# Two last token chunks of a linear map go through the weights together, and one block of stored weight combinations is dropped

## The chip, the cores and the metric

The kernel runs on one NeuronCore of a Trainium2 chip. TensorE (PE in the profile) multiplies, VectorE (DVE) and ScalarE (ACT) empty its PSUM banks and prepare operands, GpSimd (POOL) does a little elementwise work, and SyncE (SP) issues every DMA. The metric is the device time in microseconds (us); less is better.

## The reference, cut to what matters

Three parts follow each other: an attention that is linear in the sequence, a first mixture of plain matrix products, and a second mixture of four experts.

```python
# attention, 4 batches x 8 heads x 576 x 64; x becomes 2304 tokens x 512
q_s, k_s = softmax(q, axis=-1), softmax(k, axis=2)
x = einsum(q_s, einsum(k_s, v))
# first mixture: w1, w2 512x1024, w3 1024x1024, w_out 1024x512
x = ((x @ w1) * (x @ w2)) @ w3 @ w_out
# second mixture: 4 experts, w1 4x512x1024, w2 4x1024x512
p = domain_probs / domain_probs.sum(-1)
out = sum(p[:, e] * (relu(x @ w1[e]) @ w2[e]) for e in range(4))
```

## The kernel before, in words

Every fp32 operand of a product is held as two halves, a rounded high part and the rest (`split`: ScalarE writes the high part, L102, then VectorE the low part, L103), and each product is three matmuls (`mm3`, L107 to L109).

**First mixture.** The 2304 tokens are cut into five chunks, 0 to 3 of 512 tokens and 4 of 256. The 1024 inner columns are cut into NF = 8 slices f. `ab_step(c, f)` computes the two products of chunk c with slice f of w1 and w2, 12 matmuls each, into two banks of the pool `ps_w`; ScalarE copies the first out (L476, tile `ah`) and VectorE multiplies the second onto it (L477). `h_step` splits that product. `y_step(c, f)` multiplies it with slice f of `Wg` = w3 @ w_out into four accumulators `y`, 12 matmuls; these live in the four banks of the pools `ps_y`. `y_out(c)` copies them out at the end of a chunk (L508) and stores them in DRAM as `yd` (L511). The products of chunks 0 and 1 are computed early, between attention work; their `y_step`s run in 16 slots from Y0. Chunks 2, 3 and 4 follow, each with eight slices of `ab_step`, `h_step` and the `y_step` of the slice before; attention work of the last batch is put between the slices of chunk 2. The split slices of w1 and w2 are kept in DRAM, and `load_w12(c, f)` reads them again (tile `wg`, two DMAs of 512 KB, L447) for each chunk from 1 on, two slices ahead. They come from the pool `gran` of 28 buffers, which also holds x, h, ah, yt and Wg.

**Second mixture.** It is computed in three passes over the tokens, each of NGE = 8 blocks n (an expert's half of the inner columns). A block's two layers use a seven-product scheme: `layer1(n)` has 84 matmuls of 384 columns (L847) in seven steps, `layer2(n)` 126 of 256 columns (L921). The seven right-hand combinations of each layer's weights (e_a, e_s for layer 1, e_b, e_t for layer 2) are formed once. Those of layer 2, and of layer 1 for the blocks n < NE1, are formed ahead by the generator `cooking`, whose steps are taken by `cook_some(k)` during the first mixture: a block's raw weights come in by two DMAs (`load_e`, L573, tiles e1r and e2r), eleven steps make seven combinations (tiles `eo`, NOUT = 5 buffers; sums on L577, splits on L102 and L103), and each is stored in DRAM (L597). `load_cooked` reads them back (tile `eg`, pool of 9 buffers, L658). For the other blocks of layer 1, `get_e1(n)` forms the combinations in the first pass itself, among the work of the layer before, from raw weights held in `rp2`, and stores them for the later passes. `load_y` and `tset` prepare the left-hand token combinations of a pass (tiles yp and t). The pool `rp2` is opened after `gran` is closed, as are the other pools of the second mixture but yp, tok and e.

**Order.** The program is traced in the order in which the Python runs, which gives each instruction its priority. A planner then fixes the order on every engine at build time from its own timeline; it may move an instruction ahead of earlier ones if its inputs and a buffer are there. On the chip each engine and the SP queue work through their list in that fixed order.

Of the kernel before, what the change touches and what calls it, by code (L numbers as in the profile page):

```python
# [11 lines left out]
ACTF = mybir.ActivationFunctionType  # L12
# [3 lines left out]
PSUM = bass.MemoryType.PSUM  # L16
# [15 lines left out]
AB0, AB1, W1, Y0, Y1, REST = 6, 14, 22, 30, 38, 46  # L32
# [22 lines left out]
def linear_attention_moe_kernel(ctx: ExitStack, tc, q, k, v, w1, w2, w3, wo, dp, e1, e2, out):  # L55
    nc = tc.nc
# [3 lines left out]
    NF = w1.shape[1] // 256  # L60
    E = e1.shape[0]
    P = 128
# [2 lines left out]
    chunks = [(j, min(CH, NT - j)) for j in range(0, NT, CH)]  # L65
    NC = len(chunks)
    KR, KX = 4, S - 4 * P
    NE1, NOUT = 2, 5
    QP, QR = 64, 9
    HALF = S // 2  # L70
    NG, NR = 28, 4
# [10 lines left out]
    ps_y = [ctx.enter_context(tc.tile_pool(name=f"ps_y{i}", bufs=2, space=PSUM)) for i in range(2)]  # L82
    ps_w = ctx.enter_context(tc.tile_pool(name="ps_w", bufs=2, space=PSUM))

    def gran(name):
        return gp.tile([P, 2, 512], F32R, tag="g", name=name)

    def raw(name, pool=gp):
        return pool.tile([P, 1024], F32, tag="g", name=name)

    def bank(pool, name):
        return pool.tile([P, 512], F32, tag="b", name=name)
# [8 lines left out]
    def split(hi, lo, src, eng=nc.vector):  # L101
        i = nc.scalar.activation(out=hi, in_=src, func=ACTF.Copy)  # L102
        eng.tensor_tensor(out=lo, in0=src, in1=hi.bitcast(F32), op=ALU.subtract)  # L103
        return i

    def mm3(ps, w_hi, w_lo, r_hi, r_lo, first, last):
        nc.tensor.matmul(out=ps, lhsT=w_hi, rhs=r_hi, start=first, stop=False)  # L107
        nc.tensor.matmul(out=ps, lhsT=w_hi, rhs=r_lo, start=False, stop=False)  # L108
        nc.tensor.matmul(out=ps, lhsT=w_lo, rhs=r_hi, start=False, stop=last)  # L109

    gate = {}

# [47 lines left out]
    att = ExitStack()  # L160
# [189 lines left out]
    before, mid, after = {}, {}, {}  # L350

    def put(d, slot, f, *a):
        d.setdefault(slot, []).append((f, a))

    def run(d, slot):
        for f, a in d.pop(slot, []):
            f(*a)

    for b in range(B):
        for j in range(2):  # L360
            s = Q_SLOT[b][j]
# [6 lines left out]
        for i, hp in enumerate(PAIRS):  # L368
            s = K_SLOT[b][i]
# [17 lines left out]
    w12, w12d = {}, {}  # L387
# [56 lines left out]
    def load_w12(c, f):  # L444
        for i in range(2):
            g = gran("wg")
            gate["dma"] = [nc.sync.dma_start(out=g.bitcast(F32), in_=w12d[f, i])]  # L447
            w12.setdefault((c, f), []).append(g)

    def finish_lo(g, ps):  # L450
        nc.tensor.matmul(
            out=ps, lhsT=nident, rhs=g[:, 0], start=False, stop=True, skip_group_check=True
        )
        nc.scalar.activation(out=g[:, 1], in_=ps, func=ACTF.Copy)


    hg, yps, Wg, prods = {}, {}, {}, {}

    def ab_step(c, f):
        n = chunks[c][1]  # L460
        gw = w12[c, f]
        pss = []
        if f % 2 == 0:
            prods[c, f // 2] = gp.tile([P, 2, 512], F32, tag="g", name="ah")
        ah = prods[c, f // 2][:, f % 2, 0:n]
        for i in range(2):
            ps = bank(ps_y[i] if c == 0 and f % 2 else ps_w, "ab")
            for x, kt in enumerate(PAIRS):
                o = P * kt
                mm3(  # L470
                    ps[:, 0:n], gw[i][:, 0, o:o + P], gw[i][:, 1, o:o + P],
                    xa.at(c, kt, 0), xa.at(c, kt, 1), x == 0, x == KT - 1,
                )
            pss.append(ps)
            if i == 0:
                nc.scalar.activation(out=ah, in_=ps[:, 0:n], func=ACTF.Copy)  # L476
        nc.vector.tensor_tensor(out=ah, in0=pss[1][:, 0:n], in1=ah, op=ALU.mult)  # L477


    def h_step(c, f):  # L480
        n = chunks[c][1]
        h = gran("h")
        split(h[:, 0, 0:n], h[:, 1, 0:n], prods[c, f // 2][:, f % 2, 0:n])
        if f % 2:
            del prods[c, f // 2]
        hg[c, f] = h

    def y_step(c, f):
        n = chunks[c][1]
        if f == 0:  # L490
            for d in range(KT):
                yps[d] = bank(ps_y[d // 2], f"y{d}")
        h = hg.pop((c, f))
        for d in range(KT):
            o = P * d
            mm3(
                yps[d][:, 0:n], Wg[f][:, 0, o:o + P], Wg[f][:, 1, o:o + P],
                h[:, 0, 0:n], h[:, 1, 0:n], f == 0, f == NF - 1,
            )

    yd = dr.tile([P, KT, NT], F32, name="yd")
# [1 line left out]
    def y_out(c):  # L503
        j0, n = chunks[c]
        for dd in range(2):
            t = raw("yt").rearrange("p (k f) -> p k f", k=2)
            for k in range(2):
                nc.scalar.activation(  # L508
                    out=t[:, k, 0:n], in_=yps[2 * dd + k][:, 0:n], func=ACTF.Copy
                )  # L510
            nc.sync.dma_start(out=yd[:, 2 * dd:2 * dd + 2, j0:j0 + n], in_=t[:, :, 0:n])  # L511

    def x_free(c):
        for kk in list(xa.t):
            if kk[0] == c:
                del xa.t[kk]
# [59 lines left out]
    def minus(dst, x, y, op=ALU.subtract):  # L576
        return lambda: nc.vector.tensor_tensor(out=dst, in0=x, in1=y, op=op)  # L577
# [52 lines left out]
    def load_y(p):  # L630
        y = yp_.tile([P, KT, 2, TC], F32, tag="yp", name="yp")
        nc.sync.dma_start(
            out=y, in_=yd[:, :, 2 * TC * p:2 * TC * (p + 1)].rearrange("p k (t n) -> p k t n", t=2)
        )
        yraw[p] = y

    def tset(p):
        y = yraw.pop(p)
        b11, b12, b21, b22 = y[:, 0:2, 0], y[:, 0:2, 1], y[:, 2:4, 0], y[:, 2:4, 1]
        t = tok[p] = {}  # L640

        def part(name, src):
            def do():
                t[name] = tp.tile([P, 2, 2, TC], F32R, tag="t", name="t")
                split(t[name][:, :, 0], t[name][:, :, 1], src)
            return do

        return [
            part("b11", b11), part("b21", b21),
            minus(b11, b12, b11), minus(b12, b22, b12),  # L650
            part("b22", b22), minus(b22, b22, b11),
            part("t2", b22), part("t1", b11), part("t3", b12),
            minus(b21, b21, b22), part("t4", b21),
        ]

    def load_cooked(kind, n, name):
        g = ep.tile([P, 2, 2, 256], F32R, tag="e", name="eg")
        nc.sync.dma_start(out=g.bitcast(F32), in_=ewd[kind, n % NGE, name])  # L658
        ew[kind, n, name] = g

    def slot(s, *steps):
        run(before, s)
        for f, *args in steps:
            f(*args)
            run(mid, s)
        run(mid, s)
        run(after, s)
# [49 lines left out]
    save_w12(NF - 2)  # L717
    save_w12(NF - 1)
    load_w12(1, 0)
    load_w12(1, 1)  # L720
    for f in range(NF):
        if f + 2 < NF:
# [14 lines left out]
    kitchen = ExitStack()  # L737
# [3 lines left out]
    def cook_some(k):  # L741
        for _ in range(k):
            next(cooks, None)

    for i, (c, f) in enumerate(steps):
        if c == 1 and f >= NF - 2:
            load_w12(2, f - NF + 2)
        if i + 4 < len(steps):
            h_step(*steps[i + 4])
        slot(Y0 + i, (y_step, c, f))  # L750
        cook_some(2)
        if f == NF - 1:
            y_out(c)


    put(before, REST + NF * (NC - 4), load_probs)
    put(after, REST + NF * (NC - 4) + 2, probs)
    for c in range(2, NC):
        for f in range(NF):
            s = NF * (c - 2) + f  # L760
            if s < NF * (NC - 2) - 2:
                load_w12((s + 2) // NF + 2, (s + 2) % NF)
            run(before, REST + s)
            ab_step(c, f)
            h_step(c, f)
            cook_some(3)
            run(mid, REST + s)
            if f > 0:
                y_step(c, f - 1)
            cook_some(2)  # L770
            run(after, REST + s)
        x_free(c)
        y_step(c, NF - 1)
        y_out(c)
        if c == NC - 3:
            att.close()
            yp_ = ctx.enter_context(tc.tile_pool(name="yp", bufs=1, side="right"))
            tp = ctx.enter_context(
                tc.tile_pool(name="tok", bufs=7, side="right", reuse_waits="tile")
            )  # L780
        if c == NC - 2:
            cook_some(200)
            kitchen.close()
            load_y(0)
            for g in tset(0):
                g()
            ep = ctx.enter_context(
                tc.tile_pool(name="e", bufs=9, side="right", reuse_waits="tile")
            )
            for name in USE["e1"]:  # L790
                load_cooked("e1", 0, name)
    gran_stack.close()
    Wg.clear()

# [238 lines left out]
```

## Time and profile before

| what | value |
|---|---|
| median of 3 runs | 1186.36 us (1184.99 to 1188.56) |
| profiled execution | 1184.92 us, of which the span from first to last instruction is 1183.1 us |
| granted TensorE clock, mean | 0.991 |
| PE busy | 1130.7 us (96% of the span), 7048 matmuls |
| PE weight loads | 1051.4 us (89%) |
| DVE busy | 866.8 us (73%) |
| ACT busy | 535.8 us (45%) |
| DMA | 322.18 MB, mean 272 GB/s |

Busy shares are means over the whole span. A matmul's shown duration is longer than its distance to the next one, since matmuls are pipelined; the pace is read from the starts. What an idle engine waited for is inferred from semaphores.

### The profile page before, as it was taken

To read this page: it belongs to the slowest core of one execution; us is meant where nothing else is said; L and a number is where in the kernel's file an instruction comes from. 1 tells how busy PE (TensorE), PEld (TensorE's weight loads), DVE (VectorE), ACT (ScalarE), POOL (GpSimd) and SP (SyncE) were. 2 spreads that over 40 slices of the span, in tenths; PEclk is the share of its full clock that TensorE was granted. 3 is DMA by queue.
4 is the path that set the end of the run, shared out by engine and by line. 5 is a ranking of instruction groups with operands and counts; after the bars stand their busy time and mean duration, and the time that the engine had idled before them with its cause. 6 is when DMAs were issued, how large, how long until landed. Compare 5 with 4: busy or idle time off the path is not lost.

```text
span 1183.1 us, 18802 instructions
## 1 busy us (share of the span) xinstructions
PE 1130.7 (96%) x7048; PEld 1051.4 (89%) x7048; DVE 866.8 (73%) x1428; ACT 535.8 (45%) x982; POOL 50.5 (4%) x70
## 2 busy tenths in 40 slices
PE   5889999989998998999999999999999999999997
PEld 3667888778787898999999999999999999999997
DVE  6997867776467421799989987777779777777776
ACT  4665535555435322555555554434445344443441
POOL 0011300012001000000000000000000000000000
PEclk9989999999999999999999999999999999999999
DMA  9999950699899985778786789777777787777773
GB/s 231 266 350 298 361 204 21 246 365 412 305 392 344 367 337 204 270 285 286 276 288 252 257 290 316 263 251 250 249 250 244 258 297 257 251 251 251 247 252 99
DMA packets 130730, 322.18 MB, mean 272 GB/s; under 512 B 32336, under 2 KB 53328, under 8 KB 130640
## 3 DMA queue, kind: packets, MB, share of 16 engines
q1 hardware_dynamic: 130640, 320.98, 78.9%
q8 instruction: 56, 0.92, 0.3%
q14 instruction: 34, 0.28, 0.1%
HBM read 244.39 MB, written 76.55 MB: 271 GB/s over the span
## 4 chain that ended last, share of the span: by engine, by line
PE 81%; DMA 8%; DVE 5%; SPq 2%; ACT 2%; issue 1%; DVEq 0%; ACTq 0%
PE hp L847 29%; PE op L921 27%; PE ab L107 5%; PE ab L109 4%; PE ab L108 4%; DMA kr<-in_k_dram 2%; PE y L108 2%; PE y L107 2%; PE y L109 2%; DVE acc L905 1%; DMA eg<-e_a 1%; PE kv L244 1%; PE W L107 1%; PE W L108 1%; PE W L109 1%
## 5 line engine op out<-in xcount | busy, mean ns | idle before, releaser
L921 PE MATMUL op<-eg,h 128*128 128x256 f32 x3024 | 377.5, 280 | 1.4 <-DMA eg<-e_b 1.3
L847 PE MATMUL hp<-t,eg 128*128 128x384 f32 x2016 | 373.8, 336 | 2.3 <-DMA eg<-e_a 1.7
L921 PEld LDWEIGHTS op<-eg,h 128*128 128x128 f32 x3024 | 371.5, 188 | 1.9 <-issue 1.6
L847 PEld LDWEIGHTS hp<-t,eg 128*128 128x128 f32 x2016 | 345.0, 188 | 3.7 <-ACT blk L836 1.8
L905 DVE SCALAR_TENSOR_TENSOR acc<-op,prob,acc 128x256 f32<-128x256 f32 (+1 forms) x396 | 196.5, 525 | 45.8 <-PE op L921 45.4
L102 ACT ACTIVATE h<-blk 128x768 fp32r<-128x768 f32 x168 | 137.8, 842 | 142.7 <-DVE blk L577 108.8
L103 DVE TENSOR_TENSOR h<-blk,h 128x768 fp32r<-128x768 f32 x168 | 157.1, 949 | 26.9 <-ACT h L102 26.9
L830 ACT ACTIVATE blk<-hp 128x384 f32<-128x384 f32 x192 | 91.2, 490 | 147.7 <-PE hp L847 145.6
L107 PE MATMUL ab<-x,wg 128*128 128x512 f32 (+1 forms) x320 | 123.0, 386 | 8.7 <-DMA wg<-w 4.0
L834 DVE TENSOR_TENSOR blk<-hp,blk 128x384 f32<-128x384 f32 x144 | 79.5, 555 | 69.8 <-PE hp L847 67.5
L108 PE MATMUL ab<-x,wg 128*128 128x512 f32 (+1 forms) x320 | 120.8, 377 | 0.2 <-ACT x L346 0.2
L109 PE MATMUL ab<-x,wg 128*128 128x512 f32 (+1 forms) x320 | 120.2, 378 | 0.6 <-DVE wg L103 0.6
L836 ACT ACTIVATE blk<-blk 128x768 f32<-128x768 f32 x72 | 60.8, 846 | 74.1 <-DVE blk L834 72.3
L577 DVE TENSOR_TENSOR blk<-blk 128x768 f32<-128x768 f32 x96 | 91.2, 950 | 0.6
L107 PEld LDWEIGHTS ab<-x,wg 128*128 128x128 f32 x320 | 62.0, 195 | 20.3 <-DMA wg<-w 4.2
L109 PEld LDWEIGHTS ab<-x,wg 128*128 128x128 f32 x320 | 61.7, 193 | 11.7 <-DVE wg L103 1.3
L108 PEld LDWEIGHTS ab<-x,wg 128*128 128x128 f32 x320 | 62.1, 194 | 11.0 <-ACT x L346 1.2
L103 DVE TENSOR_TENSOR eo<-e2r,eo 128x512 fp32r<-128x512 f32 x56 | 39.2, 706 | 40.7 <-ACT eo L102 40.7
L477 DVE TENSOR_TENSOR ah<-ab,ah 128x512 f32<-128x512 f32 (+1 forms) x40 | 25.4, 634 | 52.2 <-PE ab L109 43.1
L108 PE MATMUL y<-h,W 128*128 128x512 f32 (+1 forms) x160 | 58.4, 372 | 3.3 <-DVE h L103 3.3
L109 PE MATMUL y<-h,W 128*128 128x512 f32 (+1 forms) x160 | 57.7, 371 | 0.0
L107 PE MATMUL y<-h,W 128*128 128x512 f32 (+1 forms) x160 | 52.0, 373 | 1.0 <-ACT h L102 1.0
(91 smaller groups left out, 1010.4 us busy)
## 6 DMA issues: line engine op xcount, KB each, us to landing
eg<-e_t SPq DMA_DIRECT2D x96, 512.0 KB, 4.7
eg<-e_s SPq DMA_DIRECT2D x72, 512.0 KB, 4.5
eg<-e_b SPq DMA_DIRECT2D x72, 512.0 KB, 5.1
wg<-w SPq DMA_DIRECT2D x64, 512.0 KB, 9.4
eg<-e_a SPq DMA_DIRECT2D x54, 512.0 KB, 4.8
f<-in_moe_w_dram SPq DMA_DIRECT2D x32, 512.0 KB, 6.7
e_t<-eo SPq DMA_DIRECT2D x32, 512.0 KB, 7.5
e_b<-eo SPq DMA_DIRECT2D x24, 512.0 KB, 8.6
```

The costliest lines, as they stand in the source:

```text
L102: i = nc.scalar.activation(out=hi, in_=src, func=ACTF.Copy)
L103: eng.tensor_tensor(out=lo, in0=src, in1=hi.bitcast(F32), op=ALU.subtract)
L107: nc.tensor.matmul(out=ps, lhsT=w_hi, rhs=r_hi, start=first, stop=False)
L108: nc.tensor.matmul(out=ps, lhsT=w_hi, rhs=r_lo, start=False, stop=False)
L109: nc.tensor.matmul(out=ps, lhsT=w_lo, rhs=r_hi, start=False, stop=last)
L577: return lambda: nc.vector.tensor_tensor(out=dst, in0=x, in1=y, op=op)
L830: nc.scalar.activation(out=block(name)[:, u], in_=src, func=func)
L834: nc.vector.tensor_tensor(out=x[:, u], in0=src, in1=x[:, u], op=ALU.add)
L836: nc.scalar.activation(out=x, in_=x, func=ACTF.Relu)
L847: nc.tensor.matmul(out=q, lhsT=w[:, sw, kt, P * u:P * u + P], rhs=t[b][:, kt, st], start=new and kt == 0 and i == 0, stop=kt == 1 and i == ...
L905: nc.vector.scalar_tensor_tensor(out=dst, in0=src, scalar=prob[:, T, e:e + 1], in1=dst, op0=ALU.mult, op1=ALU.add,)
L921: nc.tensor.matmul(out=q[:, c:c + DH], lhsT=g[:, sh, u, P * i:P * i + P], rhs=w[:, sw, u], start=new and u == 0 and j == 0, stop=u == 1 an ...
```

## The change

Three things. (1) Chunks 3 and 4 go through the slices together: `load_w12` is called for chunk 3 alone and its buffers are used by `ab_step(3, f)` and `ab_step(4, f)`, then come `y_step(3, f - 1)` and `y_step(4, f - 1)`. Chunk 4's four accumulators are pairs of halves of two banks of a new PSUM pool `ps_z`, opened when the attention's pool is closed. (2) NE1 is 1: block 1's layer-1 combinations are no longer stored ahead, but formed during `layer1(0)` like those of the blocks after it, and the raw weights of blocks 1 and 2 are the first two reads into `rp2`. (3) The steps of `cook_some` are spread otherwise: none in the first three slots from Y0, four a slice in chunk 2 and eight a slice in the joint chunks; the kitchen is closed at slice 5 of the joint chunks, and yp, tok and e are opened there, with `tset(0)` dealt out over slices 5 to 7 and the first seven `load_cooked` at slice 6.

```diff
@@ -65,7 +65,7 @@
     chunks = [(j, min(CH, NT - j)) for j in range(0, NT, CH)]
     NC = len(chunks)
     KR, KX = 4, S - 4 * P
-    NE1, NOUT = 2, 5
+    NE1, NOUT = 1, 5
     QP, QR = 64, 9
     HALF = S // 2
     NG, NR = 28, 4
@@ -103,10 +103,11 @@
         eng.tensor_tensor(out=lo, in0=src, in1=hi.bitcast(F32), op=ALU.subtract)
         return i
 
-    def mm3(ps, w_hi, w_lo, r_hi, r_lo, first, last):
-        nc.tensor.matmul(out=ps, lhsT=w_hi, rhs=r_hi, start=first, stop=False)
-        nc.tensor.matmul(out=ps, lhsT=w_hi, rhs=r_lo, start=False, stop=False)
-        nc.tensor.matmul(out=ps, lhsT=w_lo, rhs=r_hi, start=False, stop=last)
+    def mm3(ps, w_hi, w_lo, r_hi, r_lo, first, last, shared=False):
+        kw = {"skip_group_check": True} if shared else {}
+        nc.tensor.matmul(out=ps, lhsT=w_hi, rhs=r_hi, start=first, stop=False, **kw)
+        nc.tensor.matmul(out=ps, lhsT=w_hi, rhs=r_lo, start=False, stop=False, **kw)
+        nc.tensor.matmul(out=ps, lhsT=w_lo, rhs=r_hi, start=False, stop=last, **kw)
 
     gate = {}
 
@@ -446,6 +447,8 @@
             g = gran("wg")
             gate["dma"] = [nc.sync.dma_start(out=g.bitcast(F32), in_=w12d[f, i])]
             w12.setdefault((c, f), []).append(g)
+        if c == NC - 2:
+            w12[NC - 1, f] = w12[c, f]
 
     def finish_lo(g, ps):
         nc.tensor.matmul(
@@ -454,7 +457,7 @@
         nc.scalar.activation(out=g[:, 1], in_=ps, func=ACTF.Copy)
 
 
-    hg, yps, Wg, prods = {}, {}, {}, {}
+    hg, yps, Wg, prods, ps_z = {}, {}, {}, {}, []
 
     def ab_step(c, f):
         n = chunks[c][1]
@@ -487,15 +490,21 @@
 
     def y_step(c, f):
         n = chunks[c][1]
-        if f == 0:
+        pair = c == NC - 1
+        if f == 0 and pair:
+            for dd in range(2):
+                t = bank(ps_z[0], f"z{dd}")
+                for k in range(2):
+                    yps[c, 2 * dd + k] = t[:, 256 * k:256 * k + n]
+        elif f == 0:
             for d in range(KT):
-                yps[d] = bank(ps_y[d // 2], f"y{d}")
+                yps[c, d] = bank(ps_y[d // 2], f"y{d}")[:, 0:n]
         h = hg.pop((c, f))
         for d in range(KT):
             o = P * d
             mm3(
-                yps[d][:, 0:n], Wg[f][:, 0, o:o + P], Wg[f][:, 1, o:o + P],
-                h[:, 0, 0:n], h[:, 1, 0:n], f == 0, f == NF - 1,
+                yps[c, d], Wg[f][:, 0, o:o + P], Wg[f][:, 1, o:o + P],
+                h[:, 0, 0:n], h[:, 1, 0:n], f == 0 and not (pair and d % 2), f == NF - 1, pair,
             )
 
     yd = dr.tile([P, KT, NT], F32, name="yd")
@@ -506,7 +515,7 @@
             t = raw("yt").rearrange("p (k f) -> p k f", k=2)
             for k in range(2):
                 nc.scalar.activation(
-                    out=t[:, k, 0:n], in_=yps[2 * dd + k][:, 0:n], func=ACTF.Copy
+                    out=t[:, k, 0:n], in_=yps[c, 2 * dd + k], func=ACTF.Copy
                 )
             nc.sync.dma_start(out=yd[:, 2 * dd:2 * dd + 2, j0:j0 + n], in_=t[:, :, 0:n])
 
@@ -748,47 +757,67 @@
         if i + 4 < len(steps):
             h_step(*steps[i + 4])
         slot(Y0 + i, (y_step, c, f))
-        cook_some(2)
+        if i > 2:
+            cook_some(2)
         if f == NF - 1:
             y_out(c)
 
 
-    put(before, REST + NF * (NC - 4), load_probs)
-    put(after, REST + NF * (NC - 4) + 2, probs)
-    for c in range(2, NC):
-        for f in range(NF):
-            s = NF * (c - 2) + f
-            if s < NF * (NC - 2) - 2:
-                load_w12((s + 2) // NF + 2, (s + 2) % NF)
-            run(before, REST + s)
+    put(before, REST + NF, load_probs)
+    put(after, REST + NF + 2, probs)
+    for f in range(NF):
+        load_w12((f + 2) // NF + 2, (f + 2) % NF)
+        run(before, REST + f)
+        ab_step(2, f)
+        h_step(2, f)
+        cook_some(2)
+        run(mid, REST + f)
+        if f > 0:
+            y_step(2, f - 1)
+        cook_some(2)
+        run(after, REST + f)
+    x_free(2)
+    y_step(2, NF - 1)
+    y_out(2)
+    att.close()
+    two = ExitStack()
+    ps_z.append(two.enter_context(tc.tile_pool(name="ps_z", bufs=2, space=PSUM)))
+    for f in range(NF):
+        if f + 2 < NF:
+            load_w12(3, f + 2)
+        run(before, REST + NF + f)
+        for c in (3, 4):
             ab_step(c, f)
             h_step(c, f)
-            cook_some(3)
-            run(mid, REST + s)
+            cook_some(4)
+        run(mid, REST + NF + f)
+        for c in (3, 4):
             if f > 0:
                 y_step(c, f - 1)
-            cook_some(2)
-            run(after, REST + s)
+        run(after, REST + NF + f)
+        if f == NF - 3:
+            cook_some(200)
+            kitchen.close()
+            yp_ = ctx.enter_context(tc.tile_pool(name="yp", bufs=1, side="right"))
+            tp = ctx.enter_context(
+                tc.tile_pool(name="tok", bufs=7, side="right", reuse_waits="tile")
+            )
+            ep = ctx.enter_context(
+                tc.tile_pool(name="e", bufs=9, side="right", reuse_waits="tile")
+            )
+            load_y(0)
+            first_tok = tset(0)
+        if f >= NF - 3:
+            for g in first_tok[4 * (f - NF + 3):4 * (f - NF + 4)]:
+                g()
+        if f == NF - 2:
+            for name in USE["e1"]:
+                load_cooked("e1", 0, name)
+    for c in (3, 4):
         x_free(c)
         y_step(c, NF - 1)
         y_out(c)
-        if c == NC - 3:
-            att.close()
-            yp_ = ctx.enter_context(tc.tile_pool(name="yp", bufs=1, side="right"))
-            tp = ctx.enter_context(
-                tc.tile_pool(name="tok", bufs=7, side="right", reuse_waits="tile")
-            )
-        if c == NC - 2:
-            cook_some(200)
-            kitchen.close()
-            load_y(0)
-            for g in tset(0):
-                g()
-            ep = ctx.enter_context(
-                tc.tile_pool(name="e", bufs=9, side="right", reuse_waits="tile")
-            )
-            for name in USE["e1"]:
-                load_cooked("e1", 0, name)
+    two.close()
     gran_stack.close()
     Wg.clear()
```

## Rows read from the trace of the kernel before

**Rows 1.** The page: the DMA traffic of the whole program

```profile
DMA packets 130730, 322.18 MB, mean 272 GB/s; under 512 B 32336, under 2 KB 53328, under 8 KB 130640
```

**Rows 2.** Windows by stage: length, busy us by engine, granted clock, DMA share, GB/s

```profile
240.00:250.00 10.00, 6.55 (x24) 4.71 (x25) 7.73 (x16) 7.19 (x18) 3.07 (x5) 0.83 1.00 342
357.00:418.00 61.00, 57.80 (x255) 47.20 (x253) 36.31 (x56) 25.05 (x43) 5.50 (x8) 1.00 0.93 348
390.00:400.00 10.00, 10.00 (x46) 8.29 (x45) 3.16 (x5) 1.91 (x4) 0.00 (x0) 1.00 1.02 417
418.00:465.00 47.00, 41.92 (x316) 40.95 (x315) 7.41 (x18) 9.09 (x23) 0.00 (x0) 0.96 0.72 271
465.00:480.00 15.00, 15.00 (x88) 15.00 (x88) 4.31 (x7) 7.32 (x15) 0.00 (x0) 1.00 0.92 317
480.00:490.00 10.00, 8.68 (x58) 8.39 (x57) 8.51 (x12) 6.01 (x12) 0.00 (x0) 1.00 0.80 307
```

**Rows 3.** Waits of PE, 205 to 500 us: total us, times, longest

```profile
PE ab L107 <- DMA wg<-w: 4.0, 1, 4.0
PE xp L325 <- ACT bd L256: 3.4, 1, 3.4
PE y L108 <- DVE h L103: 3.3, 2, 1.9
PE op L921 <- DMA eg<-e_b: 1.3, 1, 1.3
PE ab L107 <- ACT ah L476: 1.3, 1, 1.3
PE y L107 <- ACT h L102: 1.0, 1, 1.0
```

**Rows 4.** Chain that ended last, 400 to 490 us: start, us, what

```profile
407.73 0.91 PE y L107 x4
...
428.10 8.56 DMA eg<-e_a
...
436.72 11.53 DMA wg<-w
...
455.80 0.48 PE y L107 x4
...
465.07 11.49 PE hp L847 x66
```

**Rows 5.** Timeline of PE from the longest wait: start, us, what

```profile
448.30 0.38 PE L107 MATMUL ab<-x,wg 128*128 128x256 f32 x1 [4.04 <-DMA wg<-w]
...
451.81 0.41 PE L109 MATMUL ab<-x,wg 128*128 128x256 f32 x1
```

**Rows 6.** Timeline of SP, the issues around the end of chunk 4

```profile
427.63 0.90 SPq L658 DMA_DIRECT2D eg<-e_a  x2
...
432.84 2.88 SPq L658 DMA_DIRECT2D eg<-e_a  x3
436.72 8.07 SPq L447 DMA_DIRECT2D wg<-w  x6
...
465.08 0.92 SPq L511 DMA_DIRECT2D yd<-yt  x2
...
468.59 2.54 SPq L573 DMA_DIRECT2D e1r<-in_moe_w_dram  x4
```

**Rows 7.** Groups by line: busy us, mean ns | idle before, releaser

```profile
L102 ACT ACTIVATE eo<-e2r 128x512 fp32r<-128x512 f32 x56 | 34.0, 625 | 9.4 <-DMA e_s<-eo 7.9 <-DMA e_a<-eo 1.4
...
L103 DVE TENSOR_TENSOR eg<-e1r,eg 128x512 fp32r<-128x512 f32 x42 | 28.4, 681 | 0.1
...
L477 DVE TENSOR_TENSOR ah<-ab,ah 128x512 f32<-128x512 f32 (+1 forms) x40 | 25.4, 634 | 52.2 <-PE ab L109 43.1 <-ACT ah L476 4.8 <-ACT t L102 3.8
...
L577 DVE TENSOR_TENSOR e1r<-e1r 128x512 f32<-128x512 f32 x32 | 23.5, 736 | 0.1
```

**Rows 8.** DMA issues by line: count, KB each, median us to landing

```profile
e1r<-in_moe_w_dram SPq DMA_DIRECT2D x16, 512.0 KB, 6.3
```

More of the change, by code (lines that the diff above doesn't have):

```diff
@@ L750, in linear_attention_moe_kernel @@
         slot(Y0 + i, (y_step, c, f))
-        cook_some(2)
+        if i > 2:
+            cook_some(2)
         if f == NF - 1:
             y_out(c)
-    put(before, REST + NF * (NC - 4), load_probs)
-    put(after, REST + NF * (NC - 4) + 2, probs)
-    for c in range(2, NC):
-        for f in range(NF):
-            s = NF * (c - 2) + f
-            if s < NF * (NC - 2) - 2:
-                load_w12((s + 2) // NF + 2, (s + 2) % NF)
-            run(before, REST + s)
+    put(before, REST + NF, load_probs)
[22 more added lines that the diff above has]
+        for c in (3, 4):
             ab_step(c, f)
             h_step(c, f)
-            cook_some(3)
-            run(mid, REST + s)
+            cook_some(4)
+        run(mid, REST + NF + f)
+        for c in (3, 4):
             if f > 0:
                 y_step(c, f - 1)
-            cook_some(2)
-            run(after, REST + s)
-        x_free(c)
-        y_step(c, NF - 1)
-        y_out(c)
-        if c == NC - 3:
-            att.close()
+        run(after, REST + NF + f)
+        if f == NF - 3:
+            cook_some(200)
+            kitchen.close()
             yp_ = ctx.enter_context(tc.tile_pool(name="yp", bufs=1, side="right"))
@@ L789, in linear_attention_moe_kernel @@
             )
+            load_y(0)
[4 more added lines that the diff above has]
+        if f == NF - 2:
             for name in USE["e1"]:
                 load_cooked("e1", 0, name)
+    for c in (3, 4):
+        x_free(c)
+        y_step(c, NF - 1)
+        y_out(c)
+    two.close()
     gran_stack.close()
```

## The prediction

> **What bounds the kernel now.** First the page and the table above: PE is busy 96% of the span, and the number of its matmuls is not changed. So the change can win only what PE loses between 217 us, where the combinations begin, and about 490 us, where the second mixture has found its step. Next the windows by stage: from 418 to 465 us, chunk 4's own stretch, PE is busy 41.92 of 47 us at a granted clock of 0.96, while DMA is the full engine wherever weights are read and combinations stored together: a share of 1.02 at 417 GB/s from 390 to 400 us [rows 2]. Then the waits of PE: the six largest from 205 to 500 us come to 14.3 us; the reader is to see that nearly each has another releaser and that the longest, 4.0 us, is a wait for the DMA of w1 or w2 [rows 3]. Then the chain that ended last, which tells whose fault that was: the weights' read follows directly on a read of `eg` [rows 4], and the SP timeline shows it: nine reads of `eg`, the first combinations of the second mixture, were issued from 427.63 to 432.84 us, and only after them the last six reads of `wg` [rows 6]. At 524 KB each the nine are 4.7 MB, 11.3 us at 417 GB/s, and the chain waits 11.53 us for the weights behind them.
>
> **The change, part by part.**
>
> *The shared read.* Sixteen reads of `wg` go, 8.4 MB of the 322.18 MB [rows 1]. The wait of 4.04 us has nothing left that could cause it: the last `wg` of chunk 3 is used by both chunks, and is asked for two joint slices ahead. A joint slice is 36 matmuls of 512 columns and 36 of 256. Four take 0.91 and 0.48 us [rows 4], so 8.2 + 4.3 = 12.5 us; two slices are 25 us against a read of about 12 us in the worst row. **-4.0 us.** Behind the wait the clock was down: 17 matmul distances from 448.30 to 451.81 us took 3.51 us [rows 5] where 17 x 0.12 = 2.04 us is the full pace. **-1.5 us.** Chunk 4 alone is also a short loop: its `y_step` waited 1.03 us for the split of its own product [rows 3]; joint, another chunk's 3 to 8 us of matmuls stand between. **-1.0 us.**
>
> *Is there DMA time in the joint slices?* A block's eleven steps move nine times 524 KB, 4.7 MB. Eight steps and one slice of w1 and w2 make 3.4 + 1.05 = 4.5 MB in 12.5 us, 358 GB/s; before, five steps and the same 1.05 MB in 8.2 us asked for 390 GB/s. The row at 417 GB/s [rows 2] has room for it. The Trainium skill (SBUF — State Buffer, Summary: rules for kernel authors) says to count on about 358 GB/s between HBM and SBUF. By that page there would be no room at all, a wait like the old one would come back, and the sum below would be 4.0 us higher. The row is above it, so I go by the row.
>
> *The new banks.* Within a joint slice the second product of chunk 4 needs the bank that VectorE must empty of chunk 3's second product, and only chunk 4's first product lies between: 12 x 0.12 = 1.44 us, where before a `y_step` and a whole product lay there, 5.5 us. The multiply takes 0.634 us; with one combination of 0.736 us ahead of it on VectorE it is 1.37 us and hidden, with two it is 2.1 us and PE waits 0.7 us [rows 7]. Six slices carry such steps: 0 to 4.0 us, one wait taken. VectorE was busy 36.31 of 61 us in chunk 3 [rows 2], so two in a row should be rare. **+0.7 us.** The new accumulators themselves cost nothing: as many matmuls, and the two banks were the attention's.
>
> *The moved steps.* 110 steps become 99. Fewer and later ones stand in front of the attention work and of the splits that `y_step` waits for. Before, waits of this sort cost 3.4 + 1.4 us between 217 and 245 us (the second part of the 3.3 us for `h`, less its longest, 1.9) [rows 3], and the clock of 0.83 from 240 to 250 us adds 10 x 0.17 = 1.7 us [rows 2]: 6.5 us. The planner may still move the steps forward into idle time, so they may stay, or one more of 3.4 us come. Between -6.5 and +3.4; I take **-2.0 us**, since the steps' number falls by a fifth there (26 for 32). The longest wait for `h`, 1.9 us, lies in chunk 3, where I read `tset` on VectorE ahead of it; `tset` is now dealt over three slices. Between 0 and -1.9, **-1.0 us**.
>
> *The seam.* This is the price. Block 1's combinations were stored ahead; now they start from a raw read that may begin only when `gran` is free, so after the last `yd` is stored. Before, that read was issued 468.59 - 465.07 = 3.5 us after PE turned from the last `y` to L847 [rows 4, 6], and no product waited for it. Its landing takes 6.3 us [rows 8], its second half is issued some 0.6 us later: raw weights at +10.4 us. Seven splits of 0.681 and four sums of 0.736 us are 7.7 us of VectorE [rows 7]; the third combination that `layer1(1)` uses, s2, is the tenth of eleven made: about +18. PE has `layer1(0)`, 84 matmuls at 11.49/66 = 0.174 us [rows 4], to +14.6, and two steps of `layer1(1)`, 24 matmuls, to +18.8. That just meets if VectorE is free. It was busy 4.31 of the first 15 us, but 8.51 of the next ten [rows 2]; so some 4 us of its work is put back, and `layer2(0)` waits on it. Against this stands that PE already waited 1.3 us there for `e_b` [rows 3]. What is late next is the split of `layer1(0)`'s result. Lower bound 0; upper bound, 4.2 us put back, a read 2 us late and a fallen clock of 1.5 us: 7.7 us. I take **+2.5 us**, nearer the lower end because two layers can fill each other's gaps. Traffic falls by 3.7 MB there: seven reads are saved, the seven stores are only moved.
>
> **The sum.** -4.0 - 1.5 - 1.0 + 0.7 - 2.0 - 1.0 + 2.5 = -6.3 us from the profiled 1184.92: 1178.6 us. The median of the runs is 1.44 us above the profiled one: **1180 us**. With all bounds to one side it is -15 or +9 us.
>
> **The rivals.**
>
> *The seam takes it back* (0.17). At 7.7 us for the 2.5 the time is 1185. For it: a chain of store, read, eleven steps in line with no second copy. Against it: VectorE's idle 10.7 us of the first 15.
>
> *No room on the DMA* (0.05). If the joint slices' 358 GB/s are not to be had beside the stores, one wait like the old 4.0 us comes back: 1184 us. Against it: 417 GB/s [rows 2]. It is the case that the page on SBUF speaks for.
>
> *Slower: the steps hold the banks* (0.11). ScalarE and VectorE take their lists in order. If an `eo` split of theirs waits for a buffer, that is for a store to land, chunk 3's products stand in `ps_w` behind it, and with only 1.44 us of cover PE stands too. For it: an `ab` did wait 1.3 us for ScalarE's copy `ah` [rows 3], and splits of `eo` waited 9.4 us in all, nearly all for stores [rows 7]. At 1.3 us in each of eight slices, and with no gain at the other waits: 1186.4 - 6.5 + 2.5 + 10.4 = 1193 us. It decides from about 0.95 us a slice. Against it: 7.9 of the 9.4 us is owed to `e_s`, the first blocks; later the stores kept up. The Trainium skill (PSUM — Partial Sum Buffer, Engine vs sequencer instructions) calls the queues of ScalarE and VectorE strictly first in, first out, which is what would make it happen; the `xp` that waited 3.4 us for ScalarE's `bd` [rows 3] agrees.
>
> *More than the sum* (0.16). The waits of 3.4, 1.4 and 1.9 us all go and the seam costs nothing: 1186.4 - 6.5 - 6.5 - 1.9 + 0.7 = 1172 us. For it: less of everything in that stretch. Against it: the planner fills by its own timeline.
>
> *No effect*: the weights' read was late only because `eg` was read early; if the planner again moves those seven reads in front of the last `wg`, 3.7 MB or 9 us delay a read that has 25. That is hidden, so this case is inside the forecast.
>
> **How the numbers follow.** Forecast 0.51, from 1176 to 1183. About 0.3%, 3.6 us, is what a measurement of this kernel can tell from no change: faster is below 1182.8, slower above 1189.9. Nearly all of the forecast and all of "more" are faster: 0.64. The seam and DMA rivals and the forecast's edge are the same: 0.24. The bank rival, and a seam beyond its price, are slower: 0.12. The range from 1173 to 1189 leaves out the far end of "more" and the slow side.
>
> **What would show it.** Right: no PE wait for `wg` in the last two chunks; full clock there; 48 issues of `wg` instead of 64; the first `e1r` of the second mixture some 3.5 us after the last `y`, and a wait of PE of a few us at most between +14 and +25 us. Wrong: waits of `ab` for `ah` in every joint slice, a wait of `hp` for `eg` from L103 of over 5 us with the clock down, or new waits of attention work between 217 and 357 us.

## The result, and the profile after

The changed kernel took 1176.26 us (median of 4 runs, 1173.77 to 1177.03), the kernel before, on the same chip, 1185.68 us: a ratio of 0.9912, with a 95% interval from 0.9889 to 0.9936. That is faster by 0.9%, just inside the lower end of the forecast's own range of 1176 to 1183 and 4 us below the predicted 1180. The profiled execution took 1177.03 us with a span of 1175.3; that is 7.9 us less than the profiled one of before, where the medians differ by 9.4.

The page's DMA line answers to [rows 1]: 12.06 MB fewer, which is 23 times 524 KB, the sixteen reads of `wg` and seven reads of stored combinations that the prediction counts.

```profile
DMA packets 127418, 310.12 MB, mean 264 GB/s; under 512 B 31968, under 2 KB 52960, under 8 KB 127328
```

The windows by stage, with the columns of [rows 2]; the second fence has two rows of before that [rows 2] lacks.

```profile
217.00:291.00 74.00, 68.60 (x297) 55.09 (x295) 50.90 (x91) 41.36 (x87) 11.28 (x13) 0.93 0.94 352
240.00:250.00 10.00, 6.29 (x19) 4.45 (x19) 8.48 (x18) 7.48 (x19) 3.06 (x5) 0.64 1.04 348
250.00:260.00 10.00, 10.00 (x38) 8.02 (x38) 5.24 (x9) 4.58 (x10) 0.20 (x1) 0.85 1.07 397
...
357.00:418.00 61.00, 59.71 (x342) 52.50 (x342) 29.97 (x50) 22.50 (x42) 4.85 (x8) 1.00 0.89 325
418.00:465.00 47.00, 47.00 (x276) 42.51 (x275) 7.82 (x14) 11.69 (x25) 0.00 (x0) 1.00 0.13 46
```

```profile
217.00:291.00 74.00, 68.86 (x309) 55.58 (x308) 53.80 (x92) 42.05 (x89) 14.26 (x15) 0.98 0.95 352
...
250.00:260.00 10.00, 10.00 (x46) 8.18 (x45) 6.92 (x15) 5.28 (x12) 0.20 (x1) 1.00 1.08 389
```

The gain stands in the last two rows of the first fence. From 357 to 465 us PE is busy 106.7 of 108 us, against 99.7 before [rows 2], and the granted clock is 1.00 throughout. Its first three rows show what was not gained: from 217 to 291 us PE is busy 68.60 us, against 68.86 before, and the clock is lower (0.64 and 0.85 in the two short windows, against 0.83 and 1.00).

The waits of PE from 205 to 500 us answer to [rows 3].

```profile
PE xp L326 <- ACT bd L257: 3.7, 1, 3.7
PE y L109 <- DVE h L103: 1.4, 1, 1.4
PE ab L108 <- ACT ah L479: 1.3, 1, 1.3
PE op L950 <- DMA eg<-e_b: 0.8, 1, 0.8
```

Gone are the 4.0 us for `wg`, the 1.9 us for `h` in chunk 3 and the 1.0 us for `h` in chunk 4. The waits of 3.4 and 1.4 us in the slots from Y0 stand as before. By the chain that ended last, PE turned to the second mixture's first long run of products (L876 here, L847 before) 6.3 us earlier, at 458.77 us instead of 465.07 [rows 4], with the same twelve of them already done.

```profile
458.77 15.77 PE hp L876 x90
```

The timeline of SP around the weights and the seam answers to [rows 6].

```profile
393.43 1.02 SPq L448 DMA_DIRECT2D wg<-w  x2
394.49 1.50 SPq L667 DMA_DIRECT2D eg<-e_a  x2
400.33 1.74 SPq L667 DMA_DIRECT2D eg<-e_s  x4
402.12 0.43 SPq L667 DMA_DIRECT2D eg<-e_a  x1
403.22 1.29 SPq L448 DMA_DIRECT2D wg<-w  x2
...
462.05 2.02 SPq L582 DMA_DIRECT2D e1r<-in_moe_w_dram  x4
```

The planner again put seven reads of `eg` in front of the last two reads of `wg`, but at 394 to 402 us, where the weights had two joint slices of time; nothing waited. The raw weights of block 1 are asked for 462.05 - 458.77 = 3.3 us after PE's turn, where the prediction had 3.5.

### The profile page after: what moved, and what is told of

Its sections match the earlier page's. It is cut to its first block, busy times and chain, and to the rows that moved or that the text cites. A ratio compares the mean times of both kernels' runs of the same rounds, so it can differ in the third digit from the quotient of the medians.

```text
span 1175.3 us, 18720 instructions
## 1 busy us (share of the span) xinstructions
PE 1132.6 (96%) x7048; PEld 1053.3 (90%) x7048; DVE 866.1 (74%) x1428; ACT 534.8 (46%) x982; POOL 49.4 (4%) x70
## 4 chain that ended last, share of the span: by engine, by line
PE 86%; DVE 4%; DMA 4%; ACT 1%; SPq 1%; issue 1%; DVEq 0%; ACTq 0%
PE hp L876 29%; PE op L950 27%; PE ab L108 6%; PE ab L109 6%; PE ab L110 6%; PE y L108 2%; PE y L109 2%; PE y L110 2%; PE kv L245 1%; DVE acc L934 1%; DMA qr<-in_q_dram 1%; DMA eg<-e_b 1%; PE W L108 1%; PE W L109 1%; PE W L110 1%
## 5 line engine op out<-in xcount | busy, mean ns | idle before, releaser
L876 PE MATMUL hp<-t,eg 128*128 128x384 f32 x2016 | 376.8, 336 | 0.9 <-DVE acc L934 0.9
L876 PEld LDWEIGHTS hp<-t,eg 128*128 128x128 f32 x2016 | 344.6, 188 | 2.8 <-DVE acc L934 1.9
L109 PE MATMUL y<-h,W 128*128 128x512 f32 x128 | 50.9, 399 | 1.4 <-DVE h L103 1.4
L102 ACT ACTIVATE h<-ah 128x512 fp32r<-128x512 f32 (+1 forms) x40 | 22.8, 589 | 64.0 <-DVE ah L480 64.0
L110 PE MATMUL y<-h,W 128*128 128x512 f32 x128 | 50.2, 398 | 0.0
```

The source lines that it names most:

```text
L876: nc.tensor.matmul(out=q, lhsT=w[:, sw, kt, P * u:P * u + P], rhs=t[b][:, kt, st], start=new and kt == 0 and i == 0, stop=kt == 1 and i == ...
```

## The experiments

All twelve were timed against the kernel before on the same chip. The first four, the next four and the last four each shared a chip, and the kernel before had medians of 1185.78, 1184.59 and 1186.08 us there. Runs of different groups are compared by their ratios.

### The joint slices alone

```diff
 # the changed kernel
-    NE1, NOUT = 1, 5
+    NE1, NOUT = 2, 5
```

> The changed kernel with NE1 = 2 again: the joint slices alone, block 1's combinations stored ahead and read back, 110 steps instead of 99. Theory (the gain is the joint slices': no read of w1 and w2 behind the reads of eg, no chunk 4 alone): 1175 to 1178 us, no PE wait for wg, and the seam as in the kernel before. Rival (the smaller number of combinations gave a good part of it, by less DMA and fewer splits in the way): 1179 to 1182 us, with new waits of PE between 291 and 418 us.

1174.64 us, ratio 0.9914 [0.9896, 0.9933]: all of the gain, with two blocks still stored ahead. There is no wait for `wg` and none for `h` in the last chunks; PE waits 1.9 us for `e_b` at the seam, against 1.3 us before [rows 3] and 0.8 us in the changed kernel. So one block fewer shows no gain on top of the joint slices, within intervals of about 0.2%, and PE's wait at the seam is not longer with it.

### One block fewer alone

```diff
 # the kernel before
-    NE1, NOUT = 2, 5
+    NE1, NOUT = 1, 5
```

> The kernel before with NE1 = 1 and nothing else: chunk 4 alone with its own reads. Theory: the seven reads of eg still go in front of the last reads of wg, so PE still waits 3 to 4 us for wg and the clock still falls; the seam costs 0 to 3 us: 1184 to 1188 us. Rival (fewer combinations were the gain): 1178 to 1181 us.

1179.83 us, ratio 0.9953 [0.9934, 0.9971]. I had expected the wait for `wg` to stay; it went. The last combinations are stored earlier, so the seven reads of `eg` go out from 397.00 to 407.88 us, and the last ten reads of `wg`, issued together from 427.23 us on, have none in front of them. The waits of 1.9 and 1.0 us for `h` stay, and a new one of 1.1 us of `ab` for `ah` comes at 426.65 us. The two parts of the change each remove the same wait: their gains do not add.

### The order of the reads alone

```diff
 # the kernel before
-        nc.sync.dma_start(out=g.bitcast(F32), in_=ewd[kind, n % NGE, name])
+        hold(behind, nc.sync.dma_start(out=g.bitcast(F32), in_=ewd[kind, n % NGE, name]))
...
+            if s == NF * (NC - 2) - 2:
+                for name in USE["e1"]:
+                    load_cooked("e1", 0, name, "dma")
...
-            for name in USE["e1"]:
-                load_cooked("e1", 0, name)
```

The seven reads of `eg` for the first block are traced once the last weights of chunk 4 have been asked for, and held behind the last of those reads in the queue. Two more reads of `eg`, which stood in front of the weights too, follow them.

> The kernel before with only the order of reads changed: the first seven reads of eg are traced behind the last read of wg and held behind it. All traffic, the sixteen reads of chunk 4 too, stays. If the wait of 4.0 us came from the queue's order, it and the slow clock behind it (1.5 us) go: about 1180 us, and the rest of the gain needs the joint slices. If it came from the amount of traffic, a wait for wg of over 2 us stays and the time is 1183 us or more. A late eg could cost up to 2 us at the first product of the second mixture.

1175.65 us, ratio 0.9927 [0.9907, 0.9946], with all 322.18 MB of traffic kept and five chunks done one after the other. The timeline of SP shows the new order: ten reads of `wg`, then the `eg`.

```profile
428.16 7.50 SPq L447 DMA_DIRECT2D wg<-w  x10
436.57 1.60 SPq L658 DMA_DIRECT2D eg<-e_a  x2
439.14 5.33 SPq L658 DMA_DIRECT2D eg<-e_s  x4
445.43 2.87 SPq L658 DMA_DIRECT2D eg<-e_a  x3
```

The DMA was busier from 418 to 465 us than before (305 GB/s for 271), and yet no product waited for weights. That decides it: the wait of before came from the place of the `eg` reads in the one queue, not from how much was read. I had expected about 1180 us and the rest only from the joint slices; the median is some 4 us lower than that. The profile does not place these 4 us, since the profiled run was the slowest of the six (1180.48 us).

### Joint slices in which each chunk reads its own weights

```diff
 # the changed kernel
-        if c == NC - 2:
-            w12[NC - 1, f] = w12[c, f]
...
-        if f + 2 < NF:
-            load_w12(3, f + 2)
+        if f + 1 < NF:
+            load_w12(3, f + 1)
+            load_w12(4, f + 1)
```

Chunk 2's last two slices ask only for the first joint slice, so that both chunks' reads run one slice ahead instead of two; the buffers allow no more.

> The changed kernel in which each of the two joint chunks reads w1 and w2 for itself, so that the 8.4 MB are read again; as the pool has no more room, both are read one slice ahead instead of two. If the gain is the joint order and not the saved traffic: 1175 to 1179 us and no PE wait for wg over 0.5 us. Rival (the saved traffic is the gain, the joint slices have no room on the DMA): waits for wg come in several slices, 1180 us or more.

1179.77 us, ratio 0.9951 [0.9934, 0.9969], some 4.6 us behind the changed kernel by the ratios. No product waits for `wg`; the loss lies in the waits behind ScalarE and VectorE. Window and PE timeline of this run:

```profile
357.00:418.00 61.00, 56.14 (x316) 48.56 (x315) 28.73 (x48) 21.08 (x39) 9.46 (x8) 1.00 1.00 385
```

```profile
362.77 0.39 PE L108 MATMUL ab<-x,wg 128*128 128x256 f32 x1 [1.80 <-ACT ah L477]
370.27 0.39 PE L109 MATMUL z<-h,W 128*128 128x256 f32 x1 [1.40 <-DVE h L103]
...
380.57 0.39 PE L108 MATMUL ab<-x,wg 128*128 128x256 f32 x1 [1.49 <-DVE ah L478]
```

PE is busy 56.14 of the 61 us, 3.6 us less than in the changed kernel, which is what these waits come to beyond the one of 1.29 us that the changed kernel has; and the DMA share is 1.00. In this run the rival of the banks shows in small: chunk 4's product stands still while ScalarE or VectorE has combination steps, `tset` or `yt` copies ahead of `ah`. So the version with the shared read is ahead by about 3.6 us in this window, though not through the wait that the sum gave it. Whether the traffic itself does it is not separated: the reads also run one slice less ahead, and the planner orders ScalarE otherwise (at the first of these waits a split of `eo` runs in front of `ah`, at 361.58 us, which in the changed kernel comes behind it). The window also moved 385 GB/s; the Trainium skill (SBUF — State Buffer, Summary: rules for kernel authors) says to count on about 358 GB/s, and the measured number is the one to go by.

### Two tries at the wait for bd that stayed

In the changed kernel PE waits 3.68 us for `bd`, until 244.13 us, and the granted clock is low behind it (0.64 from 240 to 250 us). First suspect: GpSimd's subtraction for the third batch; the second run moves that batch's other two operations on GpSimd as well.

```diff
 # the changed kernel, first run
 ON_VECTOR = {(x, b, i) for x in "esm" for b in range(2) for i in range(4)}
+ON_VECTOR |= {("e", 2, i) for i in range(4)}
...
 # the changed kernel, second run
-ON_VECTOR = {(x, b, i) for x in "esm" for b in range(2) for i in range(4)}
+ON_VECTOR = {(x, b, i) for x in "esm" for b in range(3) for i in range(4)}
```

> The changed kernel with one assignment more: the subtraction of the maximum from k of the third batch (line L230) runs on VectorE instead of GpSimd. The change left the wait of 3.7 us for bd at 240 us and the clock behind it as they were. Theory: the wait comes from GpSimd, as ScalarE's exponential stands in front of bd and waits for GpSimd's 2.7 us, and VectorE's split beside GpSimd takes 1.3 instead of 0.7 us; then the wait falls below 1.5 us, the clock stays at full speed from 240 to 260 us, and the time is 1168 to 1172 us. Rival: the stores hold ScalarE through the buffers of eo, whoever subtracts: a wait of 3 us or more stays, 1175 to 1178 us.

> As the run before, with also the third batch's q work (subtraction and normalisation) on VectorE instead of GpSimd. If VectorE's first sums of 2.5 us at 217 us are slow only because GpSimd works beside them, the wait of 1.4 us for the split of h at 220 us goes too: 1166 to 1171 us. Rival: VectorE takes over more than it can hide in that stretch, and other waits come: 1173 us or more.

1175.02 us, 0.9921 [0.9902, 0.9940], and 1173.47 us, 0.9911 [0.9895, 0.9926]. The wait for `bd` is 3.4 us in the first and 5.0 us in the second, where the 1.4 us wait at 220 us is gone. One part of the theory held: VectorE's split that took 1.31 us beside GpSimd's subtraction (at 241.53 us, shown further below) takes 0.67 us in the first run, at 239.09 us. But the wait stays, so GpSimd is not its cause.

### The steps begun at the first slot

```diff
 # the changed kernel
-        if i > 2:
-            cook_some(2)
+        cook_some(2)
```

> The changed kernel with the condition on the first three slots taken out, so that combinations are traced from the first slot as in the kernel before. If the later begin gives nothing (its waits at 220 and 240 us are the old ones): the changed kernel's time, 1174 to 1178 us. Rival (the later begin is worth what the prediction put on it, 2 us, and more): 1178 us or more, with a longer wait between 217 and 260 us.

1174.76 us, 0.9914 [0.9897, 0.9930], with the same two waits of 3.7 and 1.4 us. ScalarE's timeline says why: in the kernel before, in the changed kernel and in this one, exactly 16 splits of `eo` run between 205 us and the copy into `bd` at 243 us. The planner moved the steps forward into idle time, whichever slot they were written in. Here are ScalarE's `eo` splits in that stretch (length, busy us, clock, DMA share, GB/s) before and in this run; after has x16 too:

```profile
205.00:243.00 38.00, 9.71 (x16) 1.00 0.71 261
```

```profile
205.00:243.00 38.00, 9.62 (x16) 0.99 0.71 259
```

### The seam's raw weights in the other order

The raw reads of blocks 1 and 2, `ask_e1(1)` and `ask_e1(2)`, are issued in the other order, block 2's first.

```diff
 # the changed kernel
-    for n in range(NE1, NE1 + 2):
+    for n in (NE1 + 1, NE1):
         ask_e1(n)
```

> The changed kernel with the first two raw reads of the second mixture in the other order, block 2's before block 1's, so that block 1's lands some 1.3 to 2.6 us later. If the seam had 1.5 us to spare (the third combination was done 1.5 us before its product's turn), PE waits 0 to 2 us more between 475 and 490 us: 1175 to 1179 us. Rival (the seam has none to spare and the clock falls behind a long wait): 1180 us or more.

1176.20 us, 0.9932 [0.9917, 0.9947]; its interval overlaps that of the changed kernel. ScalarE's first split of block 1 starts 10.7 us after PE's turn, where the changed kernel has 7.2. The only wait of PE from 455 to 500 us is 0.31 us of `hp` for `eg`; the wait of 0.8 us for `e_b` is gone, and in the 140 us after the turn the waits for VectorE's `acc` come to 1.8 us, for 0.9. So raw weights 3.5 us later cost almost nothing: there was slack.

### The steps held behind bd, and three companions

In the trace of after, `kv` is over at 240.46 us. VectorE starts `rs` at 241.08 behind two halves of `eo`, its reciprocal at 242.76 behind a third, and ScalarE `bd` at 243.38 behind one more. The work itself is 0.15 + 0.15 + 0.61 us. VectorE and ScalarE of the changed kernel:

```profile
239.87 1.29 DVE L103 TENSOR_TENSOR eo<-e2r,eo 128x512 fp32r<-128x512 f32 x2
241.08 0.15 DVE L250 TENSOR_SCALAR rs<-kv 128x1 f32<-128x1 f32 x1
241.53 1.31 DVE L103 TENSOR_TENSOR eo<-e2r,eo 128x512 fp32r<-128x512 f32 x1 [0.30 <-ACT eo L102]
242.76 0.15 DVE L253 RECIPROCAL rs<-rs 128x1 f32<-128x1 f32 x1
```

```profile
242.32 0.63 ACT L233 ACTIVATE ek<-kr 128x512 f32<-128x512 f32 x1 [0.82 <-POOL kr L230]
242.85 0.61 ACT L102 ACTIVATE eo<-e2r 128x512 fp32r<-128x512 f32 x1
243.38 0.61 ACT L257 ACTIVATE bd<-kv,rs 64x64 f32<-64x64 f32 x2
```

So the next four runs change the order itself, the number of buffers, and both with the subtraction moved.

```diff
 # the changed kernel, in k_v: what the steps traced later are held behind
+        gate["rs"] = [i] if b == 2 else []     # i: the reciprocal
...
+            if b == 2:
+                gate["bd"] = [i]               # i: the copy into bd
 # in the generator of the steps
-                    split(g[:, 0], g[:, 1], src)
+                    hold("bd", split(g[:, 0], g[:, 1], src))
...
-                do()
+                i = do()
+                if i is not None:
+                    hold("rs", i)
```

> The kernel after, and each step of the generator is held behind the last reciprocal of rs and the last copy into bd of the third batch that stand ahead of it in the program; nothing else. Theory: the 3.68 us in which TensorE waits for bd is the combination steps' own place in the order, because the planner puts them between kv and bd: in the trace of after kv is over at 240.46, rs starts at 241.08 behind two eo halves on VectorE, the reciprocal at 242.76 behind a third one, and bd at 243.38 behind one more eo on ScalarE. The work itself is 0.15 + 0.16 + 0.61, so the wait should shrink from 3.7 to about 1 and the slow clock behind it (0.64 in 240:250, some 3 us) should go: about 1170, ratio 0.987. Rival: the attention chain of the third batch is late anyway (GpSimd's subtraction, ek), then the wait stays over 3 and the time about 1176. Second rival: the steps that are held now press the two joint chunks, with waits for ah and h of over 3 us in all in 357 to 418: 1175 or more.

> The kernel after with six buffers eo in place of five. Rival of the order as the cause of the wait for bd: ScalarE waits for a store to free a buffer (2.60 us at 237.13, 0.48 at 240.86). If the buffers are the cause, the waits of ScalarE for eo stores fall from over 10 us to under 5 in 205 to 292 and the wait for bd to under 2: about 1171. If the order is the cause, the wait for bd stays over 3 and the time about 1175.

> The steps held behind rs and bd as in the run with that alone, and the subtraction ahead of the third batch's exp on VectorE in place of GpSimd (2.68 us for the two shapes on GpSimd, 241 to 243 in the trace of after). If GpSimd is the next limit of the chain once the steps are out of it, this is faster than the hold alone by 1 us or more: 1168 to 1169. If not, the same within 1 us.

> The hold, the subtraction on VectorE and six buffers eo together, as the version meant to beat both kernels. If the three do not get in each other's way: 1167 to 1170, no wait for bd over 1.5 us, granted clock over 0.95 in 217 to 291. If held steps come late for the joint chunks: 1174 or more.

The hold alone: **1167.85 us**, ratio 0.9847 [0.9821, 0.9874], the lowest median of all; its interval lies below that of the changed kernel. Six buffers alone: 1174.20 us, 0.9912 [0.9886, 0.9937], with the wait for `bd` at 4.8 us, so the buffers are not the cause. Hold and subtraction together: 1169.66 us, 0.9864 [0.9838, 0.9890]; all three: 1169.22 us, 0.9871 [0.9844, 0.9898]. The companions add nothing to the hold; both runs show an `ab` that waits 1.8 us for `ah`, which the hold alone does not. Waits of PE from 205 to 500 us and windows of the hold alone:

```profile
PE y L109 <- DVE h L103: 1.4, 1, 1.4
PE kv L245 <- PE mt L216: 0.8, 1, 0.8
PE xp L330 <- DVE x L103: 0.6, 1, 0.6
```

```profile
217.00:291.00 74.00, 71.49 (x332) 57.80 (x331) 44.19 (x81) 36.99 (x78) 9.36 (x13) 1.00 0.75 280
240.00:250.00 10.00, 9.49 (x46) 7.48 (x45) 6.91 (x15) 7.29 (x16) 0.32 (x2) 1.00 0.82 254
...
418.00:465.00 47.00, 47.00 (x273) 43.61 (x272) 14.54 (x26) 18.32 (x36) 0.00 (x0) 1.00 0.54 196
```

The wait for `bd` is gone and the clock is 1.00 from 217 to 291 us. The steps come later, and the traffic with them: that stretch falls from 352 to 280 GB/s, and the seven reads of `eg` that the changed kernel issues from 394.49 us on go out from 415.61 us on, where it had room (46 to 196 GB/s from 418 to 465 us). Only 4 splits of `eo` run before the first `bd` of that batch, against 16.

## Why the prediction was right, and where its steps failed

**The shared read and the last chunk: right.** The sum gave -4.0, -1.5 and -1.0. Measured: the wait of 4.04 us is gone; the clock from 418 to 465 us rose from 0.96 to 1.00, 47 x 0.04 = 1.9 us; the wait of 1.03 us is gone. The cause of the longest wait was named rightly too, the `eg` reads in front of the `wg`, and the order experiment shows that their place in the queue was enough. What the prediction did not see is that three separate edits would each remove this wait.

**The longest wait for h: mis-sized.** Given as -1.0 between 0 and -1.9, it was all of 1.9 us. It stays with one block fewer and with the order alone, and is gone in the joint slices, so they removed it. PE's wait of before, then VectorE before and after:

```profile
370.27 0.50 PE L108 MATMUL y<-h,W 128*128 128x512 f32 x1 [1.91 <-DVE h L103]
```

```profile
365.44 2.69 DVE L103 TENSOR_TENSOR t<-yp,t 128x768 fp32r<-128x768 f32 x3
...
369.53 0.68 DVE L103 TENSOR_TENSOR h<-ah,h 128x512 fp32r<-128x512 f32 x1
```

```profile
366.05 0.43 DVE L103 TENSOR_TENSOR h<-ah,h 128x256 fp32r<-128x256 f32 x1 [0.48 <-ACT h L102]
366.84 1.83 DVE L103 TENSOR_TENSOR t<-yp,t 128x768 fp32r<-128x768 f32 x2 [0.36 <-ACT t L102]
```

The prediction read the cause rightly: the split of `h` stood behind `tset` (tile t). But the reason given for the gain, that `tset` is dealt over three slices, failed. Written at slices 5 to 7, `tset` still runs at 366.84 us, in the first joint slice. It no longer stands in front of a split of `h` that PE needs next: the splits of both chunks are done by then, and the next products come from the other chunk.

**The new banks: +0.7 forecast, about 0 measured.** The changed kernel has one wait of `ab` for `ah`, 1.29 us at 361.89 us, where ScalarE's four `yt` copies of chunk 2 stand in front of `ah`; before had the same wait at the same place, at 358.99 us [rows 3]. Only with the own reads, at a DMA share of 1.00, do such waits cost more, 3.6 us in all with the wait of `z`. The rival at 1193 us did not come: there is no wait of `ab` for `ah` in the later joint slices.

**The moved steps: this step failed.** The sum gave them -2.0 because "the steps' number falls by a fifth there (26 for 32)". The idle gain is 0 (3.4 + 1.4 us before, 3.7 + 1.4 after), and the profile's clock is lower behind it: 10 x 0.36 + 10 x 0.15 = 5.1 us by the two short windows against 1.7 before. The same four `xp` show what this comes to, before and after:

```profile
342.93 1.13 PE L325 MATMUL xp<-qT,bd 128*128 128x288 f32 x4
```

```profile
345.82 1.13 PE L326 MATMUL xp<-qT,bd 128*128 128x288 f32 x4
```

The changed kernel is 2.9 us late there, and was 0.1 us late at 217 us: the stretch costs 2.8 us more, where 2.0 us less were forecast. The number written per slot does not decide how many steps are in front of `bd`: it was 16 in all three versions. The size of what can be won was well read: the bound of -6.5 us for this stretch compares with the 1185.68 x (0.9912 - 0.9847) = 7.7 us that the hold won over the changed kernel, give or take some 4 us by the two intervals. The Trainium skill (PSUM — Partial Sum Buffer, Engine vs sequencer instructions), which calls the queues of ScalarE and VectorE strictly first in, first out, agrees with these rows: VectorE's reciprocal of 0.15 us starts at 242.76 us, behind a half of `eo` that took 1.31 us.

**The seam: forecast +2.5, measured about 0.** PE's first stop after its turn is the same as before, a wait for `e_b`, and smaller.

```profile
458.61 21.32 PE L876 MATMUL hp<-t,eg 128*128 128x384 f32 x120
480.77 2.35 PE L950 MATMUL op<-eg,h 128*128 128x256 f32 x18 [0.83 <-DMA eg<-e_b]
```

120 products follow without a gap. The raw read went out when the prediction said, and VectorE did more work there, as it said. Windows of the first 15 us after the turn and of the next ten, before and after:

```profile
464.91:479.91 15.00, 15.00 (x89) 15.00 (x88) 4.31 (x7) 7.32 (x15) 0.00 (x0) 1.00 0.93 316
479.91:489.91 10.00, 8.68 (x57) 8.39 (x56) 8.42 (x12) 6.01 (x12) 0.00 (x0) 1.00 0.79 307
```

```profile
458.61:473.61 15.00, 15.00 (x88) 14.79 (x87) 8.36 (x15) 10.15 (x21) 0.00 (x0) 1.00 0.79 277
473.61:483.61 10.00, 9.17 (x58) 8.67 (x57) 8.99 (x14) 7.60 (x15) 0.00 (x0) 1.00 0.98 333
```

VectorE (the third busy column) is busy 17.4 us there for 12.7. The step that failed is "some 4 us of its work is put back, and `layer2(0)` waits on it": the eleven steps fitted between VectorE's pieces of `layer1`, and PE waits for `e_b` and not for VectorE. All that shows of work put back, in the 140 us after the turn, are three waits for VectorE's `acc` of 0.9 us in all, where before has one of 0.5. A wait of 1.7 us for `e_a` later in the first pass, at 678.61 us, is gone as well.

**The sum by what was measured**, in us of the profiled executions: -4.0 - 1.9 - 1.0 - 1.9 + 2.8 (the wait for `bd` and the clock behind it) - 0.5 (`e_b`) + 0.4 (`acc`) - 1.7 (`e_a`) = -7.8, against 1177.03 - 1184.92 = -7.9. The mechanism of the larger part, the weights and the last chunk, was right. That the total of -6.3 came so close is luck: two misses, the seam's price and the steps' gain, went opposite ways by 4 to 5 us each.

**What stays open.** How much of the 2.8 us belongs to the change is not known: the kernel before has one profile only, and the mean clock differs between executions of one kernel. In the executions of the kernel before that go with the experiments it is from 0.985 to 0.992, and the time from 1188.98 down to 1180.17 us; the profiled ones had 0.991 before and 0.988 after, the lowest of the changed kernel's four. Why PE waits 1.4 us for `h` at 220 us was not pursued.

## What to carry to other kernels

When a late read ends a chain, look at what the same queue issued before it: moving the early reads behind the urgent ones was worth as much, within the intervals, as the whole change with its 23 reads fewer. Where a planner fills idle time by its own timeline, writing background work later can change nothing, as here; a dependency that holds it behind the short, urgent instruction did. And fixes of one wait are not added up: each of three edits here took the same 4 us.

## What the runs showed of the hardware

A wait's cost was more than its idle time. After the 3.68 us without a product, the changed kernel's TensorE ran at half pace: its four `xp` took 2.26 us there and 1.13 us in the kernel with the hold, that is the 1.2 and the 2.4 GHz level. Its 512-column products stood about 0.43 us apart until 252.76 us, then 0.23 to 0.24. Timeline of PE, changed kernel and hold:

```profile
244.13 2.26 PE L326 MATMUL xp<-qT,bd 128*128 128x288 f32 x4 [3.68 <-ACT bd L257]
...
252.76 0.53 PE L110 MATMUL y<-h,W 128*128 128x512 f32 x1
253.13 0.40 PE L108 MATMUL y<-h,W 128*128 128x512 f32 x1
```

```profile
240.11 1.13 PE L330 MATMUL xp<-qT,bd 128*128 128x288 f32 x4
```

What follows a wait is not in proportion to it. The granted clocks of 240 to 250 and 250 to 260 us were 0.83 and 1.00 before (after a wait of 3.4 us), 0.71 and 0.95 with the order alone (2.8), 0.64 and 0.85 in the changed kernel (3.7), 0.50 and 1.00 with the subtraction on VectorE (3.4), 0.66 and 1.00 with all three operations there (5.0). Worked out as 10 us times what each lacks to 1.00, that is a loss of 1.7, 3.4, 5.1, 5.0 and 3.4 us: the longest wait did not cost the most. With the hold, whose longest idle time from 205 to 500 us is 1.4 us, both clocks were 1.00.
